# The last matrix product by Strassen's seven products, and the cap's transfer on another queue

## The chip, the cores and the metric

One core of a Trainium2 chip runs the kernel. The metric is device time in microseconds. The five engines are TensorE (PE in the rows; PEld is its weight load), VectorE (DVE), ScalarE (ACT), GpSimd (POOL, idle here) and SyncE (SP), which issues the transfers.

## The reference, cut to what matters

```python
scores = cap * tanh(scale * q @ k^T / cap)      # 4 x 12 heads, 448 tokens, 64 wide
x = softmax(scores) @ v                         # laid out as 1792 tokens x 768
u = (x @ w1) * (x @ w2)                         # 1792 x 1024
out = (u @ w3) @ w_out                          # 1792 x 768, w3 1024 x 1024, w_out 1024 x 768
```

The weights arrive as 64-bit floats, q, k, v and the cap as 32-bit floats.

## The kernel before, in words

The kernel computes C = w3 w_out first and then out = u C. Every matrix is split into a high part (the value rounded to the type that TensorE multiplies fast) and a low part (the rest); each product is three passes, high by high, high by low and low by high.

Stages: attention per pair of heads (S: scores, tanh, exp; V: values), beside it the splitting of w1 and w2 and the products pab; u goes to DRAM as eight blocks of 128 rows by 1792 tokens. From about 373 us the weights of the tail are split (`plan_piece`, L225 to L258: nine steps a piece on VectorE and ScalarE, 16 pieces of w_out and 24 of w3). C (`plan_C`, L880) takes eight blocks `it` of 128 rows, two halves of 384 columns, eight k steps `jt` and three passes: 384 matmuls. Each block needs its three pieces of w3, for which there are four buffers (two in a tile X, two in tiles W). ScalarE writes the high part of C (L904), VectorE the low part (L908). `plan_out` takes seven groups of 256 tokens: four loads of u from DRAM (L929), the high part on ScalarE (L939), the low part on VectorE (L942), two token blocks by two halves of columns, eight k steps, three passes (L968): 672 matmuls; ScalarE copies each result out of PSUM (L988) and SP stores it (L992).

The order of the work on each engine is fixed when the program is built. A planner (`Plan`) holds every step with an engine, a cost in ns, a key and the steps that it needs. It runs a clock for each engine, takes the engine that can start first and gives it the ready step with the lowest key (ready within a short wait: 91 ns for VectorE, 119 for ScalarE). A step with an alternative (the casts that make high parts: ScalarE or VectorE) goes to the engine that comes first. The result is an order for each engine's queue; on the chip a queue goes in that order and its head waits for what it needs. The dates that matter at the start: SP is free at 600 ns, VectorE at 1300, ScalarE at 1900 (before); an SP load costs 450 and lands 3300 later; the cap's lands 2000 after its issue; the scales made from the cap cost 750 on VectorE; a cast of a pair's kq costs 890 on ScalarE or 575 on VectorE for 960 columns, the low part 1070 on VectorE; pair 0's kq comes in two cuts of 576 and 384 columns with one date. Another engine learns of a step's end 130 ns (ScalarE) or 170 ns (VectorE) later; a step with an alternative counts as another engine's. Keys at the start: pair 0's load -6, the cap's -5.5, the scales' -5, pair 0's casts and low parts 1 and 2, pair 1's load 1.3 and its cast 8.3. Buffers are slots by tag: the i-th user of a tag with n slots needs all steps of user i - n. Pieces of the tail have keys from 500 up in the order w_out, w3 (`K0`, `CK`), C from 540, C's own high and low parts 500, the output from 700.

Of the kernel before, what the change touches and what calls it, by code (L numbers as in the profile page):

```python
# [137 lines left out]
def program(  # L138
# [651 lines left out]
    JG = ((0, 3), (3, 6), (6, 8))  # L790
    K0, CK = 500, 0.72
    w3t = []

    class OutPiece(Piece):
# [8 lines left out]
        def dest(self):  # L803
            if self.jt % 2 == 0 and self.nh == 0:
                pool, tag = (wop, f"wo{self.jt}") if self.jt < KF // 2 else (big, "W")
                t = pool.tile([P, 2, 2, DM], F32R, tag=tag, name=f"wo{self.jt}")
                self.wo.update((self.jt + i, t[:, i]) for i in range(2))
            return [
                self.wo[self.jt][:, x, self.nh * NH : (self.nh + 1) * NH] for x in range(2)
            ]  # L810

    class W3Piece(Piece):
        def __init__(self, it, z):
            self.it, (self.j0, self.j1) = it, JG[z]
# [4 lines left out]
            )  # L819

        def dest(self):
            if self.j0 == 0 and self.it == 0:
# [3 lines left out]
            elif self.j0 == 0 and self.it < NW3:  # L826
                t = big.tile([P, 2 * DF], F32R, tag="W", name=f"w3y{self.it}")
                w3t.append(t.rearrange("p (x a b) -> p x a b", x=2, b=P))
            y = w3t[self.it % NW3]
# [4 lines left out]
    NW3 = 4  # L834
    ct, wo = [], {}

    def plan_wo(jt, nh):
# [3 lines left out]
            nm, OutPiece(wo, jt, nh), key, (rawb, rtb), (("rawb", 6), ("rtb", 4)), 6,  # L841
            [f"O{jt // 2 * 2}_0high"] * (jt % 2 + nh > 0),
        )
        if jt % 2 == 0 and nh == 0:
            u = plan.tag("W", KF).take(done[nm + "high"]) if jt >= KF // 2 else []
            use["wo", jt // 2] = u
        use["wo", jt // 2].extend((done[nm + "high"], done[nm + "out"]))

    def w3_users(it):
        return [use["w3t", it], use["w3y", it % NW3]]  # L850

    def plan_w3(it, z):
        i = len(JG) * it + z
        nm = f"Z{it}_{z}"
        key = K0 + (2 * KF + i) * CK
        plan_piece(
            nm, W3Piece(it, z), key, (rawb, rtb), (("rawb", 6), ("rtb", 4)), 6,
            [f"Z{it}_0high"] * (z > 0) + ["Z0_0high"] * (it == 1),
        )
        t = done[nm + "high"]  # L860
        if z == 0:
            use["w3t", it] = plan.tag("w3t", NW3).take(t)
            if it == 0:
                use["w3y", 0] = use["w3y", 1] = plan.tag("X", 2).take(t)
            elif 2 <= it < NW3:
                use["w3y", it] = plan.tag("W", KF).take(t)
        for u in w3_users(it):
            u.extend((t, done[nm + "out"]))

    def plan_C(it):  # L870
        for nh in range(2):
            ns = slice(nh * NH, (nh + 1) * NH)
            box = {}
            for jt in range(KF):

                def emit(jt=jt, box=box, nh=nh, ns=ns):
                    if jt == 0:
                        box[0] = ps_f.tile([P, 512], F32, tag="f", name=f"pc{it}_{nh}")
                    for z, (a, c) in enumerate(((0, 0), (0, 1), (1, 0))):
                        nc.tensor.matmul(  # L880
                            box[0][:, :NH],
                            lhsT=w3t[it % NW3][:, a, jt, :],
# [5 lines left out]
                key = K0 + 40 + (it * 2 + nh) * KF + jt  # L888
                z = [i for i, x in enumerate(JG) if x[0] <= jt < x[1]][0]
                t = put(  # L890
                    f"C{it}_{nh}_{jt}", "PE", 521, key, emit,
                    [f"O{jt}_{nh}high", f"O{jt}_{nh}out", f"Z{it}_{z}high", f"Z{it}_{z}out"]
                    + [f"C{it}_{nh}_{jt - 1}"],
                )
                if jt == 0:
                    f = plan.tag("f", 3).take(t)
                use["wo", jt // 2].append(t)
                for u in w3_users(it):
                    u.append(t)

            def high(ns=ns, box=box, nh=nh):
                if it % 2 == 0 and nh == 0:
                    ct.append(big.tile([P, 2, 2, DM], F32R, tag="W", name=f"c_hl{it}"))
                nc.scalar.copy(ct[it // 2][:, it % 2, 0, ns], box[0][:, :NH])  # L904

            def low(ns=ns, box=box):
                h, l = (ct[it // 2][:, it % 2, x, ns] for x in range(2))
                nc.vector.tensor_tensor(l, box[0][:, :NH], h, op=ALU.subtract)  # L908

            t = put(f"D{it}_{nh}", "ACT", 400, K0, high, [f"C{it}_{nh}_{KF - 1}"])  # L910
            f.append(t)
            if it % 2 == 0 and nh == 0:
                t.key = key
                plan.tag("W", KF).take(t)
                t.key = K0
            t = put(f"L{it}_{nh}", "DVE", 470, K0, low, [f"D{it}_{nh}"])
            f.append(t)


    def plan_out(t):  # L920

        key = K0 + 200 + 10 * t
        hl, rs = {}, {}
        bs = range(2 * t * P // S, (2 * (t + 1) * P - 1) // S + 1)
        for m in range(0, KF, 2):

            def load(m=m):
                rs[m] = rawb.tile([P, 2, 2 * P], F32, tag="raw", name=f"ru{t}_{m}")
                nc.sync.dma_start(  # L929
                    rs[m],  # L930
                    u_dr[m : m + 2, :, 2 * t * P : 2 * (t + 1) * P].rearrange(
                        "m p t -> p m t"
                    ),
                )

            def high(m=m):
                if m == 0:
                    hl[0] = xp.tile([P, 2, KF, 2 * P], F32R, tag="X", name=f"uhl{t}")
                nc.scalar.copy(hl[0][:, 0, m : m + 2, :], rs[m])  # L939

            def low(m=m):
                nc.vector.tensor_tensor(  # L942
                    hl[0][:, 1, m : m + 2, :], rs[m], hl[0][:, 0, m : m + 2, :], op=ALU.subtract
                )

            x = put(
                f"q{t}_{m}", "SP", 800, key, load,
                [f"U{b}_{m + i}" for b in bs for i in range(2)], 2500,
            )
            r = plan.tag("rawb", 6).take(x)  # L950
# [192 lines left out]
```

## Time and profile before

| | us |
|---|---|
| median of three runs | 620.69 (618.08, 622.15, 620.69) |
| profiled execution | 617.45 |
| its span, first to last instruction | 615.7 |
| TensorE busy | 595.2 (97%) |
| VectorE busy | 357.3 (58%) |
| ScalarE busy | 312.9 (51%) |

The table gives one profiled execution beside the three timed ones. A busy share is a mean over stages; the stage's own windows tell more. TensorE's granted clock is given as a share of full speed (1.00 is 2.4 GHz).

### The profile page before, as it was taken

The page shows a single profiled execution, that of the slowest core. Times are in us where ns is not written, and L with a number is a line of the kernel's source. Part 1 is how long each engine was busy: PE and PEld are TensorE (multiplying, and loading weights), DVE is VectorE, ACT ScalarE, POOL GpSimd, SP SyncE. Part 2 cuts the span into 40 slices and gives each one's busy share as a digit, 9 for nine tenths or more (in the row PEclk, how much of TensorE's full clock was granted, in tenths as well). Part 3 has the DMA queues.
Part 4 walks back from the last instruction along what each step waited for, and adds up shares of the span by engine and source line. Part 5 has one row for each costly group of instructions (what it writes and reads, how often), then busy time and mean ns, then how long its engine had stood idle before and what let it go on. Part 6 is the DMA issues. An engine that isn't in the chain of part 4 may idle for free.

```text
span 615.7 us, 8843 instructions
## 1 busy us (share of the span) xinstructions
PE 595.2 (97%) x3336; PEld 479.4 (78%) x3336; DVE 357.3 (58%) x765; ACT 312.9 (51%) x485; POOL 0.2 (0%) x4
## 2 busy tenths in 40 slices
PE   5899999999999999999999998999999999999995
PEld 3443577666579777786777777999999999999995
DVE  3679999999991254562453356999999201111100
ACT  5999976797881146564554533444545212222200
POOL 0000000000000000000000000000000000000000
PEclk9999999999999999999999999999999999999998
DMA  7335554745551032222211116555645213332111
GB/s 239 99 113 179 170 188 135 240 130 159 192 168 46 15 97 77 81 72 75 76 48 47 31 50 231 161 181 181 188 141 157 92 39 107 121 120 79 47 52 43
DMA packets 39492, 71.87 MB, mean 117 GB/s; under 512 B 6034, under 2 KB 24082, under 8 KB 39442
## 3 DMA queue, kind: packets, MB, share of 16 engines
q1 hardware_dynamic: 39442, 71.23, 36.2%
q8 instruction: 28, 0.46, 0.3%
q14 instruction: 22, 0.18, 0.1%
HBM read 58.20 MB, written 12.93 MB: 116 GB/s over the span
## 4 chain that ended last, share of the span: by engine, by line
PE 77%; ACT 10%; DVE 5%; DMA 4%; issue 1%; SPq 1%; ACTq 0%; DVEq 0%
PE pab L741 34%; PE po L968 19%; PE pc L880 11%; PE s L397 6%; PE pv L446 5%; ACT p L411 5%; ACT p L408 4%; PE pv L436 1%; PE sum L472 1%; DMA kq<-in_kq_dram 1%; DMA raw_w<-in_moe_w_dram 1%; DMA r_dr<-z 1%; DMA raw_wo<-in_moe_w_out_dram 1%; DVE hl L364 1%; ACT t_w L230 1%
## 5 line engine op out<-in xcount | busy, mean ns | idle before, releaser
L741 PE MATMUL pab<-x,w_hl 128*128 128x448 f32 x1152 | 255.2, 374 | 2.7 <-ACT x L589 2.1
L741 PEld LDWEIGHTS pab<-x,w_hl 128*128 128x128 f32 x1152 | 212.6, 188 | 44.5 <-issue 20.7
L968 PE MATMUL po<-c_hl,uhl 128*128 128x384 f32 x672 | 116.6, 334 | 0.0
L968 PEld LDWEIGHTS po<-c_hl,uhl 128*128 128x128 f32 x672 | 116.5, 188 | 0.0
L408 ACT ACTIVATE p<-s,tsc_sb 128x896 f32<-128x896 f32 (+1 forms) x96 | 84.3, 916 | 38.3 <-PE s L397 37.9
L411 ACT ACTIVATE p<-p,ncap_sb,acap_sb 128x896 f32<-128x896 f32 (+1 forms) x96 | 97.7, 1047 | 0.5
L397 PE MATMUL s<-hl 64*128 64x448 f32 (+1 forms) x504 | 77.4, 392 | 8.5 <-ACT hl L360 4.4
L397 PEld LDWEIGHTS s<-hl 64*128 64x128 f32 (+1 forms) x504 | 50.9, 189 | 37.0 <-issue 17.8
L446 PE MATMUL pv<-p,v 128*64 128x448 f32 x288 | 61.3, 551 | 0.7 <-ACT p L411 0.7
L942 DVE TENSOR_TENSOR uhl<-ru,uhl 128x512 fp32r<-128x512 f32 x28 | 17.8, 686 | 74.4 <-ACT uhl L939 74.4
L988 ACT COPY ob<-po 128x384 f32<-128x384 f32 x28 | 13.4, 478 | 92.7 <-PE po L968 84.7
L230 ACT ACTIVATE t_w<-t_w,rebias 128x384 int32<-128x384 int32 (+1 forms) x56 | 33.0, 602 | 28.9 <-DVE t_w L225 28.8
L446 PEld LDWEIGHTS pv<-p,v 128*64 128x64 f32 x288 | 17.7, 136 | 31.9 <-issue 25.4
L766 DVE TENSOR_TENSOR u<-pab,u 128x448 f32<-128x448 f32 x32 | 19.6, 613 | 39.3 <-PE pab L741 36.1
L458 DVE TENSOR_TENSOR a<-p,p 128x896 f32<-128x896 f32 x24 | 26.1, 1088 | 27.3 <-PE sum L472 18.5
L880 PE MATMUL pc<-wo,w3x 128*128 128x384 f32 x192 | 33.6, 334 | 0.0
L880 PE MATMUL pc<-wo,w3y 128*128 128x384 f32 x192 | 33.6, 334 | 0.0
L880 PEld LDWEIGHTS pc<-wo,w3x 128*128 128x128 f32 x192 | 33.4, 188 | 0.0
L880 PEld LDWEIGHTS pc<-wo,w3y 128*128 128x128 f32 x192 | 33.3, 188 | 0.0
L233 DVE SCALAR_TENSOR_TENSOR t_w<-raw_w,t_w 128x384 int32<-128x384 int32 (+1 forms) x56 | 29.1, 527 | 2.6 <-ACT t_w L230 2.5
L241 DVE SCALAR_TENSOR_TENSOR raw_w<-raw_w 128x384 f32<-128x384 uint32 (+1 forms) x56 | 29.3, 528 | 0.1
L763 ACT COPY u<-pab 128x448 f32<-128x448 f32 x24 | 12.7, 529 | 31.5 <-PE pab L741 31.4
(59 smaller groups left out, 430.3 us busy)
## 6 DMA issues: line engine op xcount, KB each, us to landing
raw_w<-in_moe_w_dram SPq DMA_DIRECT2D x48, 384.0 KB
kq<-in_kq_dram SPq DMA_DIRECT2D x23, 480.0 KB
u_dr<-u SPq DMA_DIRECT2D x32, 224.0 KB
ru<-u_dr SPq DMA_DIRECT2D x28, 256.0 KB
v<-in_v_dram SPq DMA_DIRECT2D x24, 256.0 KB
raw_wo<-in_moe_w_out_dram SPq DMA_DIRECT2D x16, 384.0 KB
r<-r_dr SPq DMA_DIRECT2D x48, 112.0 KB
out_dram<-ob SPq DMA_DIRECT2D x28, 192.0 KB
```

The lines of the kernel that those rows point to most:

```text
L230: nc.scalar.activation(self.t, self.t, AF.Relu, bias=rebias, scale=4096.0)
L233: nc.vector.scalar_tensor_tensor(self.t, self.hi, SIGN, self.t, op0=ALU.bitwise_and, op1=ALU.bitwise_or)
L241: nc.vector.scalar_tensor_tensor(self.lo.bitcast(F32), self.lo.bitcast(U32), 2.0**-32, self.hi, op0=ALU.mult, op1=ALU.add,)
L397: nc.tensor.matmul(box[0][:, j, :S], lhsT=hl[at, a, ks], rhs=hl[at, c, QO:], start=(z == 0), stop=(z == 2),)
L408: nc.scalar.activation(p_t[pr, i], box[0][:, :w, :S], AF.Tanh, scale=tsc_sb)
L411: nc.scalar.activation(p_t[pr, i], p_t[pr, i], AF.Exp, scale=acap_sb, bias=ncap_sb)
L446: nc.tensor.matmul(box[0][j * D : (j + 1) * D, :S], lhsT=v_t[pr][:, 3 * j + i - 1, :], rhs=p_t[pr, i][:, j, :], start=False, stop=(i == 3) ...
L458: nc.vector.tensor_tensor(a_t[pr], p_t[pr, 1], p_t[pr, 2], op=ALU.add)
L741: nc.tensor.matmul(box[0][:, :S], lhsT=w_t[m][:, a, wi, kt, :], rhs=x_t[b][:, c, kt, :], start=(kt == 0 and z == 0), stop=(kt == KX - 1 an ...
L766: nc.vector.tensor_tensor(box[2][0], box[1][0][:, :S], box[2][0], op=ALU.mult)
L880: nc.tensor.matmul(box[0][:, :NH], lhsT=w3t[it % NW3][:, a, jt, :], rhs=wo[jt][:, c, ns], start=(jt == 0 and z == 0), stop=(jt == KF - 1 a ...
L968: nc.tensor.matmul(box[0][:, :NH], lhsT=hl[0][:, a, m, z * P : (z + 1) * P], rhs=ct[m // 2][:, m % 2, c, ns], start=(m == 0 and i == 0), s ...
```

## The change

The output stage computes u C with one level of Strassen's scheme in Winograd's form. C is cut into four quadrants (512 rows by 384 columns), u into four (896 tokens by 512 columns). Seven products of half size replace eight. The right operands are the quadrants B11, B21, B22 and T1 = C12 - C11, T3 = C22 - C12, T2 = C22 - T1, T4 = T2 - C21; the left ones are A11, A12, A22 and S1 = A21 + A22, S2 = S1 - A11, S3 = A11 - A21, S4 = A12 - S2.

C's row blocks are now computed in the order 0, 4, 1, 5, 2, 6, 3, 7 (`ITS`), so that a row of all four quadrants is there after every second block. Each result of C is copied out of PSUM whole (`D`), VectorE makes the four sums of a row as soon as they can be made, and each of the seven operands is split in high (ScalarE or VectorE) and low part (VectorE): 28 high, 28 low, 16 sums of 384 columns, where there were 16 high and 16 low. These steps have key 499, ahead of the pieces. w3 has two buffers in place of four, the split weights' temporaries three in place of four; one more w_out tile lies outside the W tiles, because the seven operands take seven of those eight.

The output stage takes seven blocks t of 128 tokens from the upper and 128 from the lower half of the tokens: four loads (one for each quadrant of u), four sums and seven splits of 512 columns, then the products in the order 1, 5, 2, 3, 6, 7, 4, each four k steps by three passes with 384 columns. Product 2 is added in the bank of product 1 and product 3 in that of 5, after copies of these (M1, M5) on ScalarE; the other sums of products are five steps of 384 columns on VectorE. Four stores a block leave as before.

At the start the cap's transfer is issued by ScalarE in place of SP; the planner's date for ScalarE's first step is 700 ns in place of 1900, and the scales' key is 2.5 in place of -5.

```diff
+    HF = KF // 2
+    ITS = [i // 2 + i % 2 * HF for i in range(KF)]
+    NRAW, NRT, NOB, NF = 6, 3, 9, 6
...
-            use["w3t", it] = plan.tag("w3t", NW3).take(t)
+            use["w3t", n] = plan.tag("w3t", 2).take(t)
...
+    RHS = {1: "B11", 2: "B21", 3: "B22", 4: "T4", 5: "T1", 6: "T2", 7: "T3"}
+    LHS = {1: "A11", 2: "A12", 3: "S4", 4: "A22", 5: "S1", 6: "S2", 7: "S3"}
+    ORDER = (1, 5, 2, 3, 6, 7, 4)
...
+            t = put(
+                f"D{c}", "ACT", 400, K0, lambda f=evac: f(nc.scalar.copy), [f"C{n}_{nh}_{KF - 1}"],
+                0, [("DVE", 450, lambda f=evac: f(nc.vector.tensor_copy))],
+            )
...
+            t = put(
+                f"h{name}_{k}", "ACT", 412, K0 - 1, lambda: high(nc.scalar.copy),
+                [after] + ["hB11_0"] * (not first), 0,
+                [("DVE", 269, lambda: high(nc.vector.tensor_copy))],
+            )
...
+            t = put(f"l{name}_{k}", "DVE", 470, K0 - 1, low, [f"h{name}_{k}"])
...
+        if not lower:
+            split("B11", c11, f"D{c11}")
+            combine(f"T1_{k}", c11, c12, c11, [f"D{c12}", f"lB11_{k}"])
+            split("T1", c11, f"T1_{k}")
+        else:
+            split("B21", c21, f"D{c21}")
+            split("B22", c22, f"D{c22}")
+            combine(f"T3_{k}", c12, c22, c12, [f"D{c22}", f"T1_{k}"])
+            combine(f"T2_{k}", c11, c22, c11, [f"D{c22}", f"lT1_{k}"])
+            split("T2", c11, f"T2_{k}")
+            split("T3", c12, f"T3_{k}")
+            combine(f"T4_{k}", c21, c11, c21, [f"T2_{k}", f"lB21_{k}"])
+            split("T4", c21, f"T4_{k}")
...
+                ru[nm] = rawb.tile([P, HF, P], F32, tag="raw", name=f"{nm}_{t}")
+                nc.sync.dma_start(
+                    ru[nm], u_dr[b * HF : (b + 1) * HF, :, at[a]].rearrange("m p t -> p m t")
+                )
...
+        for a, b in ((0, 0), (1, 0), (1, 1), (0, 1)):
+            load_quadrant(a, b)
+        l11 = split("A11", "A11", f"q{t}A11")
+        s3 = combine("S3", "A11", "A21", ALU.subtract, [f"q{t}A11", f"q{t}A21"], new=True)
+        s1 = combine("A21", "A21", "A22", ALU.add, [s3, f"q{t}A22"])
+        split("S1", "A21", s1)
+        l12 = split("A12", "A12", f"q{t}A12")
+        s2 = combine("A11", "A21", "A11", ALU.subtract, [s1, s3, l11])
+        s4 = combine("A12", "A12", "A11", ALU.subtract, [s2, l12])
+        split("S4", "A12", s4)
+        split("S2", "A11", s2)
+        split("S3", "S3", s3)
+        split("A22", "A22", f"q{t}A22")
...
+                    for z, (a, c) in enumerate(((0, 0), (0, 1), (1, 0))):
+                        nc.tensor.matmul(
+                            box[banks[m]][:, :NH],
+                            lhsT=hl[g][:, i, a, k, :],
+                            rhs=bt[RHS[m]][:, k, c, :],
...
+        copy(f"e{t}M1", "U", "X", 1, 0)
+        copy(f"e{t}M5", "M5", "Z", 5, 1)
+        copy(f"e{t}11", "o11", "X", 2, 2)
+        store("o11", 0, 0, f"e{t}11")
+        add(f"e{t}U", "U", "Y", "U", ALU.add, [end(6), f"e{t}M1"])
+        add(f"e{t}12", "o12", "Z", "U", ALU.add, [end(3), f"e{t}U"], new=4)
+        store("o12", 0, 1, f"e{t}12")
+        add(f"e{t}V", "U", "V", "U", ALU.add, [end(7), f"e{t}12"])
+        add(f"e{t}22", "M5", "U", "M5", ALU.add, [f"e{t}V", f"e{t}M5"])
+        store("M5", 1, 1, f"e{t}22")
+        add(f"e{t}21", "U", "W", "U", ALU.subtract, [end(4), f"e{t}22"])
+        store("U", 1, 0, f"e{t}21")
...
-            nc.sync.dma_start(cap_sb, cap.to_broadcast([P, 1]))
+            nc.scalar.dma_start(cap_sb, cap.to_broadcast([P, 1]))
...
-        plan.free.update(PE=1500.0, ACT=1900.0, DVE=1300.0, POOL=900.0, SP=600.0)
+        plan.free.update(PE=1500.0, ACT=700.0, DVE=1300.0, POOL=900.0, SP=600.0)
...
-        put("cap0", "SP", 450, -5.5, load_cap, lat=2000)
-        put("cap", "DVE", 750, -5, scales, ["cap0"])
+        put("cap0", "ACT", 450, -5.5, load_cap, lat=2000)
+        put("cap", "DVE", 750, 2.5, scales, ["cap0"])
```

## Rows read from the trace of the kernel before

**Rows 1.** The page: the chain's shares; groups with count | busy us, mean ns.

```profile
PE 77%; ACT 10%; DVE 5%; DMA 4%; issue 1%; SPq 1%; ACTq 0%; DVEq 0%
L741 PE MATMUL pab<-x,w_hl 128*128 128x448 f32 x1152 | 255.2, 374 | 2.7 <-ACT x L589 2.1
```

**Rows 2.** Windows: length, busy of PE, PEld, DVE, ACT, POOL, then clock, DMA share, GB/s.

```profile
9.50:78.60 69.10, 64.53 (x417) 32.43 (x415) 56.51 (x106) 68.77 (x97) 0.00 (x0) 1.00 0.49 156
...
426.30:476.20 49.90, 49.90 (x290) 49.90 (x289) 49.38 (x141) 23.98 (x50) 0.00 (x0) 1.00 0.52 159
476.20:492.90 16.70, 16.70 (x98) 16.70 (x97) 4.69 (x8) 4.10 (x8) 0.00 (x0) 1.00 0.31 95
...
492.89:609.39 116.50, 116.49 (x673) 116.17 (x671) 13.04 (x21) 23.78 (x48) 0.00 (x0) 1.00 0.23 78
609.39:615.70 6.31, 0.00 (x0) 0.00 (x0) 0.00 (x0) 0.48 (x1) 0.00 (x0) 0.72 0.12 39
```

**Rows 3.** The chain in order of time, the tail: start, us, what.

```profile
426.31 66.58 PE pc L880 x384
492.89 116.50 PE po L968 x672
...
609.46 0.48 ACT ob L988
```

**Rows 4.** Groups by line in the tail: count | busy us, mean ns | idle before.

```profile
L942 DVE TENSOR_TENSOR uhl<-ru,uhl 128x512 fp32r<-128x512 f32 x28 | 17.8, 686 | 74.4 <-ACT uhl L939 74.4
L939 ACT CAST uhl<-ru 128x512 fp32r<-128x512 f32 x28 | 15.6, 620 | 1.9 <-DMA ru<-u_dr 1.9
...
L255 ACT CAST w3x<-t_w 128x384 fp32r<-128x384 f32 (+1 forms) x11 | 5.2, 484 | 6.1 <-DVE t_w L233 6.0
...
L255 ACT CAST w3y<-t_w 128x384 fp32r<-128x384 f32 (+1 forms) x9 | 4.3, 475 | 4.3 <-DVE t_w L233 4.2
```

**Rows 5.** VectorE in order of time, the tail: start, us, line, operation.

```profile
405.93 0.35 DVE L255 CAST wo<-t_wo 128x384 fp32r<-128x384 f32 x1
406.20 0.55 DVE L241 SCALAR_TENSOR_TENSOR raw_wo<-raw_wo 128x384 f32<-128x384 uint32 x1
...
471.29 0.55 DVE L908 TENSOR_TENSOR c_hl<-pc,c_hl 128x384 fp32r<-128x384 f32 x1
471.76 0.41 DVE L233 SCALAR_TENSOR_TENSOR t_w<-raw_w,t_w 128x256 int32<-128x256 int32 x1
472.09 0.68 DVE L942 TENSOR_TENSOR uhl<-ru,uhl 128x512 fp32r<-128x512 f32 x1
472.69 0.29 DVE L238 TENSOR_SCALAR raw_w<-raw_w 128x256 int32<-128x256 int32 x1
...
474.36 0.42 DVE L258 SCALAR_TENSOR_TENSOR w3y<-raw_w 128x256 fp32r<-128x256 f32 x1
```

**Rows 6.** The chain in order of time, the start: start, us, what.

```profile
1.65 0.42 SPq L1009
...
2.12 6.46 DMA kq<-in_kq_dram
...
9.50 0.64 ACT p L408
```

**Rows 7.** ScalarE and VectorE in order of time, the start; in brackets idle before, releaser.

```profile
3.65 1.08 ACT L360 CAST hl<-kq 128x576 fp32r<-128x576 f32 x2 [1.64 <-DMA kq<-in_kq_dram]
...
7.33 1.23 DVE L364 TENSOR_TENSOR hl<-kq,hl 128x576 fp32r<-128x576 f32 x2
...
8.60 0.99 ACT L360 CAST hl<-kq 128x960 fp32r<-128x960 f32 x1 [3.86 <-DMA kq<-in_kq_dram]
...
15.80 0.65 DVE L360 CAST hl<-kq 128x960 fp32r<-128x960 f32 x1
```

**Rows 8.** Window of the start, columns as in rows 2.

```profile
3.20:5.80 2.60, 0.74 (x1) 0.28 (x1) 0.00 (x0) 1.08 (x2) 0.00 (x0) 1.00 0.72 108
```

**Rows 9.** The chain in order of time, a load of weights: start, us, what.

```profile
368.97 4.43 DMA raw_wo<-in_moe_w_out_dram
```

More of the change, by code (lines that the diff above doesn't have):

```diff
@@ L894, in plan_C @@
                 )
                 if jt == 0:
-                    f = plan.tag("f", 3).take(t)
+                    f = plan.tag("f", NF).take(t)
                 use["wo", jt // 2].append(t)
-                for u in w3_users(it):
+                for u in (use["w3t", n], use["w3y"]):
                     u.append(t)
[L901 to L904, printed above, removed]
@@ L917, in plan_C, with evac @@
-            f.append(t)
-    def plan_out(t):
[L922 to L928, printed above, removed]
+            c = f"c{lower}{nh}_{k}"
+            def evac(cp, box=box, c=c):
+                cf[c] = obp.tile([P, NH], F32, tag="ob", name=c)
+                cp(cf[c], box[0][:, :NH])
@@ L946, in plan_out @@
+            bs = range(at[a].start // S, (at[a].stop - 1) // S + 1)
             x = put(
[L947 to L955 removed]
@@ new lines, in load_quadrant, with combine, emit @@
+                f"q{t}{nm}", "SP", 800, key, load,
+                [f"U{i}_{m}" for i in bs for m in range(b * HF, (b + 1) * HF)], 2500,
+            )
+            x.spare = SPARE
+            use[nm, t] = plan.tag("rawb", NRAW).take(x)
+        def combine(to, a, b, op, needs, new=False):
+            def emit():
+                if new:
+                    ru[to] = rawb.tile([P, HF, P], F32, tag="raw", name=f"{to}_{t}")
+                elif to != a and to != b:
+                    raise ValueError(to)
+                nc.vector.tensor_tensor(ru[to], ru[a], ru[b], op=op)
+            x = put(f"s{t}{to}{a}{b}", "DVE", 600, key, emit, needs)
+            if new:
+                use[to, t] = plan.tag("rawb", NRAW).take(x)
+            for y in {to, a, b}:
+                use[y, t].append(x)
+            return f"s{t}{to}{a}{b}"
@@ new lines, in add, with emit @@
+        def add(nm, to, bank, b, op, needs, new=None):
+            def emit():
+                if new is not None:
+                    result(to)
+                x = box[bank][:, :NH] if bank in box else ob[bank]
+                a, c = (ob[b], x) if op == ALU.subtract else (x, ob[b])
+                nc.vector.tensor_tensor(ob[to], a, c, op=op)
+            x = put(nm, "DVE", 470, key - 5, emit, needs)
+            if new is not None:
+                x.key = key + 2 * new
+                use[to, t] = plan.tag("ob", NOB).take(x)
+                x.key = key - 5
+            for y in {to, bank, b}:
+                use[y, t].append(x)
```

254 lines of the change are left out of this document (147 added, 107 removed).

## The prediction

> **What bounds the kernel now.** I began with the page: 77% of the chain that ended last is TensorE [rows 1]. The busy times by stage say where an engine's time is the kernel's time: from 426.3 us to 609.4 TensorE has no gap, while in the last of these stretches VectorE is busy 13.04 of 116.50 us and ScalarE 23.78 [rows 2]. The chain in order of time shows the two stages that the change touches as unbroken matmuls: 66.58 us for 384 of C, 116.50 us for 672 of the output, 173.4 ns each in both, then a copy and a store [rows 3]. VectorE needs a second look: it is busy 49.38 of 49.90 us up to 476.20, then 4.69 of 16.70 [rows 2]: full through most of C, with 12.0 us free at its end. The start is read apart: its chain is a transfer of kq, a cast, then tanh and exp, and ScalarE is busy 68.77 of 69.10 us from 9.50 to 78.60 [rows 6, 2], so a late first tanh is a late kernel.
>
> **The output stage.** Seven products of four k steps and three passes, for seven row blocks: 588 matmuls instead of 672, same shape (128x128 by 128x384). 84 x 173.4 ns = **14.57 us off**, if TensorE stays without gaps. The work that must keep up, per block of 84 x 173.4 ns = 14.57 us: on VectorE 7 low parts and 4 sums of 512 columns at 0.60 (start to start of such a row and the next), and 5 result sums of 384 at 0.47 [rows 5]: 6.6 + 2.35 = 8.95 us. On ScalarE 7 casts of 620 ns [rows 4] and 3 copies of 480 [rows 3]: 5.8 us. Both lie beside matmuls. SP issues four u loads and four stores a block, as many as before; the loads read 512-byte runs where they read 1 KB, with the DMA engines 0.23 busy in this stretch [rows 2]. Products 2 and 3 start in a bank that must have been copied out; another product (12 x 173.4 ns = 2.08 us) lies between, and a copy starts 0.07 us after its matmuls (609.46 against 492.89 + 116.50) and takes 0.48 [rows 3]: nothing. If that cover goes (ScalarE stuck ahead of the copy), each block pays the copy, 0.5 us. The last result is a VectorE sum (0.55 us, the row of C's low part, which also reads PSUM) in place of a copy (0.48) [rows 5, 3]: +0.07. The store behind it is the same size.
>
> **The C stage.** TensorE's 384 matmuls stay. VectorE gets 28 low parts for 16 and 16 sums that are new: 28 x 0.47 = 13.2 us. The first left parts (11 x 0.60 = 6.6) stand for 8 low parts of u (4.8): +1.8. Some high parts go to VectorE: ScalarE took 20 of the 24 casts of w3 [rows 4], VectorE the others; a sixth of 28 at 0.27 [rows 5] is 1.2. Together 16.2 against 12.0 us free: 4.2 us of work slides past the end of C. That is covered by need: of the seven right operands T2, T3 and T4 enter 8.3, 10.4 and 12.5 us into the first block. The harder date is w3's last piece, since sums go ahead of pieces in the planner's keys. It was finished at 474.78 [rows 5], and the last i block of C starts at 426.31 + 7 x 8.32 = 484.6. Ahead of it go the sums' steps of k = 0 and 1 (22) and the first three of k = 2, where 10 low parts of C had gone before: 15 more (7.0 us), and 1 us of casts, less 4 low parts of u that are no longer ahead (2.4): 480.4. Two w3 buffers instead of four mean that this block's high parts wait for 426.31 + 6 x 8.32 = 476.2, which is earlier still. Behind such a waiting high part on ScalarE stand the next piece's rebias and, behind that, VectorE's sign step; the planner knows the date, and ScalarE has room. So I take 0; margin 4.2 us. Below, the bound is 0 as well, for TensorE has no gap there to close [rows 2]; above I take 4 us, the overflow as a stall.
>
> **The start.** SP loses a 0.42 us issue that stands ahead of pair 1's kq (0.47 with the gap before it) [rows 6]. ScalarE issues it while it waits anyway: its first cast starts at 3.65 after 1.64 us of idling [rows 7]. What the move does to the order costs more than the issue. The planner decides by its own dates who casts pair 1. Before: ScalarE, free at 5.37, because kq1 is dated 5.25; the trace agrees, with the 960-column cast on ScalarE at 8.60, after two small ones [rows 7]. Now kq1 is dated 0.6 + 2 x 0.45 + 3.3 = 4.80, VectorE has done the cap's scales (3.28 to 4.03), ScalarE is busy till 4.88, and pair 0's low part is dated 5.01. So VectorE takes pair 1's cast **ahead of pair 0's low part**, and in the real run stands in its queue until kq1 lands. It landed at 8.58; 0.47 earlier at best. Then the cast, 0.65, the first low part about 0.7 (1.23 for the two) [rows 7], two score matmuls about 0.75 (twice the 374 ns of a 448-column one [rows 1]): tanh at 10.2 to 10.7 instead of 9.50. I take the middle, **+0.9**. The cast that leaves ScalarE is no second gain: it ended where tanh began. The bounds: if VectorE did pair 0's low part while it waits for the cap, and then the scales, these would end not at 7.33 but earlier by the cap's earlier issue, 1.65 against 0.73 at best, and tanh would start at about 6.5: -3.0. Upward +1.2.
>
> On the transfer itself the trace shows a stretch from 3.2 to 5.8 us, behind pair 0's load and ahead of kq1's landing, in which the DMA engines were 0.72 busy but moved 108 GB/s [rows 8], against 156 at 0.49 busy from 9.50 on [rows 2]. The cap's, issued between the two loads [rows 6], is the likely cause, and it is now issued beside pair 0's load. I take nothing for that, since kq1 was behind both before and is so now. The Trainium skill ("DMA: Bandwidth & Descriptors", Issuing engines are not separate DMA queues) says that transfers from different issuers share the same 16 engines and interleave, so that another queue saves issue time only. By that, the cap's move is worth the issue slot and no more, and its place in the order is open; this is rival 3.
>
> **Sum.** The profiled execution took 617.45 us (615.7 span, 1.75 around it): 617.45 - 14.57 + 0.07 + 0.9 + 0 = 603.9. The median of the three runs, 620.69, lies 3.24 above it; on that scale **607.1 us**.
>
> **Rivals.** *1. VectorE bounds C.* If the planner gives VectorE most of the 28 casts and half the 16 evacuations (28 x 0.27 + 8 x 0.47 = 11 us, not 1.2), the last w3 piece comes near 490 and TensorE waits about 5 us: 612. For it: VectorE is full to 476 [rows 2]. Against: ScalarE is busy only 23.98 of those 49.90 us [rows 2], and took most casts so far.
>
> *2. Slower: the preparation loop of the output stage is longer than a block.* Six raw slots hold the loads and S3 of a block, so block t+1's A21 can be loaded only when A11 of block t has been through S3, S1, S2 and S2's split, and A12 only after A22's. By durations: issue 0.4, landing at most 4.43 (a load of weights with five others behind it [rows 9]), three sums and one low part at 0.69, a cast at 0.62 [rows 4]: 8.2 us, and with the five result sums between them (2.75) 11. It is the bound from 14.57 us; over 1% slower needs 14.57 + (13.6 + 6.2)/7 = 17.4 us a block, for instance if a blocked head of VectorE's queue, a result sum waiting for TensorE, keeps the next block's preparation behind it. Then each block ends with a gap: 627 or more. Behind a waiting load on SP stand the stores, whose nine slots last two blocks. Against: the planner orders by dates, and its costs fit the trace (512-column low part 600 against 0.60 measured). A rule bears on it, in the Trainium skill ("Perfetto Trace Analysis", Optimization Strategy): a gap that repeats on the engine that should be full can mean too few buffers for the next tile. No row of before shows such a gap.
>
> *3. The cap's transfer shifts the loads.* If its small packets interleave with pair 0's load instead of standing between pair 0 and pair 1, kq1 can land earlier or later by up to the stretch in which they held the engines, 2.6 us [rows 8]; VectorE's cast waits for it, so the tanh moves with it: 604.5 or 609.7.
>
> *4. The start gains:* the -3.0 above instead of +0.9: 603.2.
>
> **Chances.** Forecast 0.70 (603 to 610), rival 1 0.12 (609 to 614), rival 2 0.06, rival 3 0.04, rival 4 0.05; the last 0.03 are gaps of 1 to 2.5 us a block, half of rival 2, 614.5 to 625. The range takes in rival 4, the forecast and most of rival 1, with about 1 us for the median of few runs: 602 to 613. A measurement of this kernel tells about 1% (6.2 us) from no change: faster by more than that 0.87, within it 0.07 (the half of rival 2, the tail of 1 and 0.02 of the forecast's own for what I don't see), slower 0.06.
>
> **What would show it.** In the profile after: 588 matmuls of the products in about 102 us without idle time, and about 66.6 us for C; if TensorE idles in C with releaser VectorE (w3's low part), rival 1; if a gap comes back with every block, rival 2, and the granted clock (1.00 in these stretches, 0.72 after the last matmul [rows 2]) should then be looked at too. At the start: a 960-column cast of kq on VectorE ahead of the first low part, and tanh after 10 us. The forecast is wrong if the products' stretch exceeds 110 us or the first tanh comes before 8.

## The result and the profile after

| | before | after |
|---|---|---|
| median of the runs, us | 621.42 (618.08 to 622.26, 4 runs) | 612.53 (611.64 to 613.37, 4 runs) |
| profiled execution, us (span) | 617.45 (615.7) | 611.64 (609.8) |

The ratio is 0.9862, 95% interval [0.9838, 0.9886]: faster by 1.4%, 8.9 us by the medians. The forecast was 607.1; the time lies inside the range of 602 to 613, at its upper end. The profiled spans differ by 5.9 us, and this is where they do: C begins 8.72 us later (435.03 against 426.31 [rows 3]), C itself takes 0.06 more, the output stage 14.56 less, and what is behind it 0.11 less. The profiled execution of the kernel before is a short one of its kind (617.45 us against medians of 620.5 to 621.5), so the spans differ by less than the medians.

The tail of the chain in order of time after (start, us, what); it answers to [rows 3] and [rows 9]:

```profile
375.73 3.12 DMA raw_wo<-in_moe_w_out_dram
379.41 0.61 ACT t_wo L230
380.50 54.53 PE pab L741 x252
435.03 66.64 PE pc L890 x384
501.66 101.94 PE m L1084 x588
603.63 0.55 DVE U L1131
```

The 588 matmuls of the products stand without a gap, 173.4 ns each, and C has none either. Ahead of C the chain goes the same way as before the change: the first load of w_out, a rebias on ScalarE (L230, a step of the splitting of the weights), a copy of pab (the first result of the last block of u) out of PSUM, and the 252 matmuls. But the copy comes 5.5 us later. Before, behind the load at 368.97 [rows 9]:

```profile
373.88 0.04 ACT t_wo L230
...
374.40 0.52 ACT u L763
```

After, the load starts at 375.73 and the rebias at 379.41. The windows (length, busy of PE, PEld, DVE, ACT, POOL, clock, DMA share, GB/s) of the entry to the tail, of C in two parts, of the output stage and of the end:

```profile
375.00:380.00 5.00, 2.25 (x6) 1.18 (x5) 0.71 (x3) 0.59 (x2) 0.00 (x0) 0.52 0.62 200
380.00:385.00 5.00, 4.50 (x12) 4.03 (x13) 3.29 (x9) 2.54 (x6) 0.00 (x0) 0.50 0.88 319
...
435.03:484.93 49.90, 49.90 (x289) 49.90 (x289) 47.23 (x129) 23.80 (x50) 0.00 (x0) 1.00 0.38 111
484.93:501.66 16.73, 16.73 (x98) 16.64 (x97) 16.73 (x41) 9.80 (x19) 0.00 (x0) 1.00 0.23 65
501.66:603.60 101.94, 101.93 (x589) 101.61 (x587) 65.45 (x116) 33.71 (x63) 0.00 (x0) 1.00 0.35 109
603.60:609.79 6.19, 0.00 (x0) 0.00 (x0) 0.55 (x1) 0.00 (x0) 0.00 (x0) 0.80 0.20 71
```

From 375 to 385 us TensorE's granted clock is 0.52 and 0.50, half speed, the lower of its two levels (1.2 GHz). The kernel before, in the same ten microseconds:

```profile
375.00:380.00 5.00, 5.00 (x25) 4.64 (x26) 3.91 (x11) 2.51 (x5) 0.00 (x0) 1.00 0.59 232
380.00:385.00 5.00, 5.00 (x26) 4.64 (x25) 5.00 (x14) 0.52 (x1) 0.00 (x0) 1.00 0.55 157
```

What TensorE waited for there, in order of time (in brackets idle before, releaser), first before, then after:

```profile
372.67 1.75 PE L741 MATMUL pab<-x,w_hl 128*128 128x448 f32 x6 [1.56 <-ACT x L589]
374.97 10.20 PE L741 MATMUL pab<-x,w_hl 128*128 128x448 f32 x49 [0.55 <-ACT u L763]
```

```profile
374.73 2.52 PE L741 MATMUL pab<-x,w_hl 128*128 128x448 f32 x6 [1.99 <-ACT x L589]
380.50 11.75 PE L741 MATMUL pab<-x,w_hl 128*128 128x448 f32 x45 [3.25 <-ACT u L763]
```

The wait for the copy of pab is 3.25 us instead of 0.55. ScalarE's rows after say why the copy is late:

```profile
379.41 0.61 ACT L230 ACTIVATE t_wo<-t_wo,rebias 128x384 int32<-128x384 int32 x1 [4.74 <-DVE t_wo L225]
379.94 0.51 ACT L763 COPY u<-pab 128x448 f32<-128x448 f32 x1
```

The copy stands in ScalarE's queue behind the rebias of w_out's first piece, where it stood before too, and that piece was loaded late: the six loads that it is the first of were issued from 375.73, right behind the last work on x (VectorE, 374.70 for 0.64), and before the change from 368.97. In the built program the first of these loads waits for TensorE alone before, and for TensorE, VectorE and four transfers after. So the 8.72 us fall into three: the last x came 2.06 later (the six matmuls on it start at 374.73, not 372.67); from there to the next matmul 5.77 us instead of 2.30, 3.47 more, all of it set by the late copy; and the 252 matmuls 54.53 us instead of 51.34, 3.19 more.

The start of the chain in order of time after, and then VectorE and ScalarE there; they answer to [rows 6, 7]:

```profile
1.67 5.40 DMA kq<-in_kq_dram
7.67 0.76 DVE hl L364
```

```profile
7.10 0.66 DVE L360 CAST hl<-kq 128x960 fp32r<-128x960 f32 x1 [1.08 <-DMA kq<-in_kq_dram]
7.67 2.29 DVE L364 TENSOR_TENSOR hl<-kq,hl 128x576 fp32r<-128x576 f32 x3
...
5.23 1.08 ACT L360 CAST hl<-kq 128x576 fp32r<-128x576 f32 x2 [2.79 <-DMA kq<-in_kq_dram]
9.63 0.64 ACT L408 ACTIVATE p<-s,tsc_sb 128x448 f32<-128x448 f32 x1 [3.32 <-PE s L397]
```

VectorE takes pair 1's 960-column cast ahead of pair 0's low part, as forecast; the first tanh is at 9.63, where 10.2 to 10.7 had been forecast. Pair 1's kq landed at 7.07 (8.58 before), pair 0's first cast began at 5.23 (3.65 before).

### The profile page after: what moved, and what is told of

Its sections match the earlier page's. It is cut to its first block, busy times and chain, and to the rows that moved or that the text cites. A ratio compares the mean times of both kernels' runs of the same rounds, so it can differ in the third digit from the quotient of the medians.

```text
span 609.8 us, 8833 instructions
## 1 busy us (share of the span) xinstructions
PE 585.6 (96%) x3252; PEld 467.7 (77%) x3252; DVE 423.3 (69%) x888; ACT 330.9 (54%) x516; POOL 0.2 (0%) x4
## 4 chain that ended last, share of the span: by engine, by line
PE 80%; ACT 8%; DMA 6%; DVE 4%; issue 1%; SPq 1%; ACTq 0%; DVEq 0%
PE pab L741 36%; PE m L1084 17%; PE pc L890 11%; PE s L397 7%; PE pv L446 6%; ACT p L411 3%; ACT p L408 3%; PE pv L436 2%; DMA r_dr<-z 2%; DMA r<-r_dr 1%; PE sum L472 1%; DMA raw_w<-in_moe_w_dram 1%; DMA kq<-in_kq_dram 1%; SPq L559 1%; DMA raw_wo<-in_moe_w_out_dram 1%
## 5 line engine op out<-in xcount | busy, mean ns | idle before, releaser
L741 PE MATMUL pab<-x,w_hl 128*128 128x448 f32 x1152 | 259.7, 378 | 6.8 <-ACT x L589 3.5
L741 PEld LDWEIGHTS pab<-x,w_hl 128*128 128x128 f32 x1152 | 214.8, 190 | 50.9 <-issue 20.7
L890 PE MATMUL pc<-wo,w3x 128*128 128x384 f32 x384 | 66.8, 334 | 0.0
L890 PEld LDWEIGHTS pc<-wo,w3x 128*128 128x128 f32 x384 | 66.6, 188 | 0.1
L1084 PE MATMUL m<-bB,lx 128*128 128x384 f32 x252 | 45.9, 334 | 0.0
L230 ACT ACTIVATE t_w<-t_w,rebias 128x384 int32<-128x384 int32 (+1 forms) x56 | 32.9, 601 | 21.4 <-DVE t_w L225 21.4
L1084 PEld LDWEIGHTS m<-bB,lx 128*128 128x128 f32 x252 | 43.9, 188 | 0.0
L1034 ACT CAST lx<-A 128x512 fp32r<-128x512 f32 x32 | 19.6, 620 | 28.6 <-DVE A L1010 11.0
L360 DVE CAST hl<-kq 128x960 fp32r<-128x960 f32 x22 | 14.4, 655 | 25.1 <-PE s L397 23.9
L1084 PE MATMUL m<-bT,lx 128*128 128x384 f32 x168 | 31.4, 334 | 0.0
L1084 PE MATMUL m<-bT,lw 128*128 128x384 f32 x168 | 30.2, 334 | 0.0
```

The source lines that it names most:

```text
L230: nc.scalar.activation(self.t, self.t, AF.Relu, bias=rebias, scale=4096.0)
L741: nc.tensor.matmul(box[0][:, :S], lhsT=w_t[m][:, a, wi, kt, :], rhs=x_t[b][:, c, kt, :], start=(kt == 0 and z == 0), stop=(kt == KX - 1 an ...
L890: nc.tensor.matmul(box[0][:, :NH], lhsT=w3t[n % 2][:, a, jt, :], rhs=wo[jt][:, c, ns], start=(jt == 0 and z == 0), stop=(jt == KF - 1 and ...
L1084: nc.tensor.matmul(box[banks[m]][:, :NH], lhsT=hl[g][:, i, a, k, :], rhs=bt[RHS[m]][:, k, c, :], start=(new and k == 0 and z == 0), stop=( ...
```

## The experiments

The theory after the result, P: the new pools (a third w_out tile, nine result buffers instead of three) push the raw weights' buffers over memory that the last attention pair still uses (among its tiles xf, from which x is made, and r); the first load then waits for that pair, the rebias for the load, the copy of pab for the rebias, and TensorE's clock falls in the wait. Rivals: Q, the place is harmless and the new order of the tail is the cause; O, the order in ScalarE's queue could hide the late load; S, the cap's move makes the start later; K, the clock's share of the loss is its own.

Each median stands beside one of the kernel before on the same chip: 620.61 for e1 to e4, 620.5 for e5 to e8, 621.5 for e9 and e10. Across these three groups, and against the changed kernel's 612.53, only the ratios compare:

| run | median, us | ratio to before, interval | C starts at |
|---|---|---|---|
| e1_pools | 608.01 | 0.9781 [0.9761, 0.9802] | 431.37 |
| e2_before_moved | 625.55 | 1.0079 [1.0057, 1.01] | 431.53 |
| e3_order | 607.87 | 0.9789 [0.9772, 0.9807] | 429.82 |
| e4_cap_back | 610.84 | 0.984 [0.9824, 0.9856] | 433.45 |
| e5_before_cap | 622.02 | 1.0029 [1.0014, 1.0043] | 427.83 |
| e6_pools_cap_back | 606.32 | 0.9779 [0.9754, 0.9804] | 431.25 |
| e7_pools_cast_act | 606.39 | 0.9778 [0.9756, 0.9799] | 431.23 |
| e8_fill | 603.8 | 0.9741 [0.9718, 0.9765] | 426.88 |
| e9_after_fill | 609.97 | 0.9822 [0.9801, 0.9842] | 431.31 |
| e10_all | 606.0 | 0.9752 [0.9731, 0.9773] | 428.12 |

**The pools opened first** (changed kernel, instruction order the same):

```
-        wop = fin.enter_context(tc.tile_pool(name="wop", bufs=1))
-        obp = fin.enter_context(tc.tile_pool(name="obp", bufs=NOB))
         rawb = ...
         rtb = ...
+        wop = fin.enter_context(tc.tile_pool(name="wop", bufs=1))
+        obp = fin.enter_context(tc.tile_pool(name="obp", bufs=NOB))
```

> The changed kernel with one edit: the pools of the raw weights and of their temporaries are opened ahead of the w_out and result pools, so that they lie over memory that attention has left long ago. The order of instructions on every engine is that of the changed kernel. Theory P (place): the first load of w_out no longer waits for the last pair's x, is issued at about 370 us and not at 375.7, TensorE's gaps between 370 and 381 fall from 6.1 us to about 2 to 3, the granted clock stays 1.00, C starts at 427 to 429 and not at 435.0; time 604 to 606, some 6 to 8 us under the changed kernel's 612.5. Rival Q (queue): SP was late in any case, because a small transfer of the softmax sums landed 1.7 us later and SP stood behind it; then the load is issued at 374 or later and the time is 610 or more.

608.01, ratio 0.9781. SyncE's and TensorE's rows of this kernel in order of time:

```profile
372.83 3.17 SPq L218 DMA_DIRECT2D raw_wo<-in_moe_w_out_dram  x6
...
376.41 15.90 PE L741 MATMUL pab<-x,w_hl 128*128 128x448 f32 x69 [2.36 <-ACT x L589]
```

The loads go out behind the last r transfer again, with no wait for x, and no wait for the copy of pab is left. 0.8% of before came back, some 5 us, less than expected: the wait for x stayed, 2.36 us, the clock in the five microseconds behind it was 0.66, and the attention itself ended 1.7 us later than in the changed kernel's trace (last sums at 364.27 against 362.54).

**The kernel before with its raw buffers pushed on:**

```
-        obp = fin.enter_context(tc.tile_pool(name="obp", bufs=3))
+        obp = fin.enter_context(tc.tile_pool(name="obp", bufs=17))
```

> The kernel before with one edit: the result pool has 17 buffers for 3, of which the plan still uses 3 at a time; nothing else, and the raw weights' pool moves to where the changed kernel has it. Theory P: the first load of w_out waits for the last x and is issued at 374 to 376 us instead of 369, TensorE's clock falls to half for a few us, C starts 5 to 8 us later, the time is 626 to 629 against about 621. Rival Q: no change, 620 to 622.

625.55, ratio 1.0079: slower, a little less than expected, with nothing changed but where the buffers lie. In the built program they lie at the addresses that they have after the change, and the first load waits for the same engines and transfers as there. Chain of this kernel in order of time, then its windows:

```profile
372.94 3.62 DMA raw_wo<-in_moe_w_out_dram
376.56 0.60 ACT t_wo L230
377.63 53.90 PE pab L741 x252
```

```profile
370.00:375.00 5.00, 2.38 (x8) 1.10 (x6) 1.25 (x2) 0.56 (x1) 0.00 (x0) 0.80 0.29 65
375.00:380.00 5.00, 2.37 (x6) 2.15 (x7) 1.51 (x5) 1.55 (x3) 0.00 (x0) 0.50 1.00 375
380.00:385.00 5.00, 5.00 (x19) 4.49 (x18) 5.00 (x14) 2.07 (x4) 0.00 (x0) 0.68 0.34 101
```

The same load, the same rebias, the same fall of the clock and slow 252 matmuls (53.90) as after the change, in a kernel without the seven products. C starts 5.22 us later. P is shown: the place alone does it. Q, by which the place is harmless, is refuted.

**The planner told of the late load** (changed kernel; the first six loads get the last x as a need, so that the planner orders ScalarE by the true date):

```
+    LATE = {f"O{j}_{h}" for j in range(3) for h in range(2)}
...
+            if st == "load" and nm in LATE:
+                need = [f"N2{NPAIR - 1}"]
```

> The changed kernel, pools where it has them, with one edit: the planner is told that the first six loads of w_out need the last pair's x. The loads stay late (375 to 376 us); ScalarE's copy of the first result of the last block of u then stands ahead of the first rebias in its queue. If the loss comes from the queue's head (the copy behind a rebias that waits for a late load), the copy runs at 376 to 377 and not at 379.9, TensorE is idle about 3 us less there, its clock falls less or not at all, and C starts at 428 to 430; time 605 to 608. If the late load itself is the loss (VectorE gets the weights late), C starts at 433 or later and the time stays at 611 or more.

607.87, ratio 0.9789. The loads are as late as in the changed kernel (376.26), but the copies now stand ahead of the rebias, and only the wait for x is left. TensorE's rows of this kernel (line numbers are three higher):

```profile
375.26 9.97 PE L744 MATMUL pab<-x,w_hl 128*128 128x448 f32 x38 [2.13 <-ACT x L592]
...
484.28 8.27 PE L893 MATMUL pc<-wo,w3x 128*128 128x384 f32 x46 [1.05 <-DVE w3x L259]
```

So what a late load costs is what stands behind it in ScalarE's queue; O holds, the order alone recovers what the place does. The second row is the forecast's rival 1 in small: TensorE waits 1.05 us in C for a late piece of w3 from VectorE.

**The cap back on SyncE's queue** (changed kernel):

```
-            nc.scalar.dma_start(cap_sb, cap.to_broadcast([P, 1]))
+            nc.sync.dma_start(cap_sb, cap.to_broadcast([P, 1]))
...
-        put("cap0", "ACT", 450, -5.5, load_cap, lat=2000)
-        put("cap", "DVE", 750, 2.5, scales, ["cap0"])
+        put("cap0", "SP", 450, -5.5, load_cap, lat=2000)
+        put("cap", "DVE", 750, -5, scales, ["cap0"])
```

> The changed kernel with the cap's transfer back on SP and the planner's dates and keys of before for it; the Strassen part stays. By my forecast the move of the cap costs about 0.9 us, so this kernel would be 611.6; by the trace the first tanh was 0.13 us later than before, so 612.4. If the other queue also slows the small transfers of the softmax sums, the first r transfers land as in the kernel before and the kernel is up to 2 us faster, 610.5. The start's order is that of before: pair 1's cast on ScalarE, tanh at 9.5 us. C starts at 433 to 435.

610.84, ratio 0.984 against 0.9862 of the changed kernel: 0.22% or 1.4 us, less than the two intervals tell apart. **The cap's move alone**, in the kernel before (the same lines the other way):

> The kernel before with nothing of the change but the cap's transfer on ScalarE's queue. Theory S (the start's order costs; taken from the changed kernel against the same with the cap back, 0.9862 to 0.9840, and from TensorE's place at the last attention sums, 101.5 us against 100.0): 1.2 to 1.6 us slower than before, 621.8 to 622.2 against 620.6, first tanh at 9.6 to 10.2 us instead of 9.50 and every later stage of the attention later by the same. Rival: the 1.4 us is chance between runs and the cap's place costs nothing: 620.3 to 621.0. Second rival: the earlier start of the first query pieces wins: under 620.

622.02, ratio 1.0029 [1.0014, 1.0043] of twelve runs: slower by 0.9 to 2.7 us. That the move costs is shown. That it costs by making the start later, as S has it, is not. VectorE's row and ScalarE's at the start of this kernel, then TensorE's at the entry to the tail, a window and the chain there:

```profile
7.21 0.66 DVE L360 CAST hl<-kq 128x960 fp32r<-128x960 f32 x1 [0.85 <-DMA kq<-in_kq_dram]
...
9.74 0.63 ACT L408 ACTIVATE p<-s,tsc_sb 128x448 f32<-128x448 f32 x1 [3.25 <-PE s L397]
```

```profile
373.05 1.75 PE L741 MATMUL pab<-x,w_hl 128*128 128x448 f32 x6 [1.56 <-ACT x L589]
...
375.00:380.00 5.00, 4.89 (x17) 4.47 (x18) 3.21 (x9) 2.11 (x5) 0.00 (x0) 0.68 0.65 257
...
375.11 52.72 PE pab L741 x252
```

The first tanh is 0.24 us later than before, the last sums of the attention 0.37 (362.65 against 362.28), and C 1.52 (427.83 against 426.31). In between the granted clock fell, behind a wait for x that is as long as before (1.56 us), and the 252 matmuls took 1.38 us more. So most of what this one execution lost is not the start's. Whether the twelve runs lost their time in the same place is open: their mean clocks (0.992 to 0.996) hardly differ from those of the seventeen beside them (0.993 to 0.996).

Over the profiled executions with that order of VectorE (after, e1, e3, e5, e9) the first tanh is at 9.63, 9.88, 9.41, 9.74 and 10.13, a mean of 9.76; with the cap on SyncE's queue (before, e2, e4, e6, e8, e10) at 9.50, 8.34, 9.47, 10.01, 8.33 and 9.58, a mean of 9.21. The two groups overlap: single profiles of the start differ by more than the move costs.

**Both undone: pools first and the cap back** (e1's edit and e4's):

> The changed kernel with the raw weights' pools opened ahead of the new ones (so that they keep off attention's last tiles) and the cap back on SP's queue. If the two costs (place of the pools 5 us, cap 1.4 us) are apart and add up: 606.4 to 606.8, C starting near 429.8 us of the span. Rival: the place and the start share a cause, or e1's later attention was the pools' order and not the cap's: 607.7 to 608.3 as with the pools alone.

606.32 is the number expected, but the ratio, 0.9779 [0.9754, 0.9804], equals e1's, and the chips differ; in its profile the first tanh came at 10.01 and C began at 431.25. That the two gains add up is neither shown nor refuted.

**Pair 1's cast kept on ScalarE, cap on ScalarE's queue, pools first:**

```
-                [("DVE", 575 * w, lambda f=high: f(nc.vector.tensor_copy))],
+                [("DVE", 575 * w, lambda f=high: f(nc.vector.tensor_copy))] * (pr != 1),
```

> As the changed kernel with the pools opened first, the cap on ScalarE's queue, but pair 1's cast kept on ScalarE, so that VectorE comes to pair 0's low part first. Theory S1 (the order of VectorE's first casts is the cost of the start): first tanh at 8.2 to 9.0 us, 606.0 to 607.0. Rival S2 (the other order at the start or the transfers' order costs, not VectorE's turn): 607.7 to 608.3, with tanh earlier and the time given back before the last attention pair.

606.39 lies in the range of S1, but on a chip where the kernel before was at 620.5; the ratio, 0.9778, is that of e1 (0.9781). VectorE's first row on kq in this kernel:

```profile
6.13 0.76 DVE L364 TENSOR_TENSOR hl<-kq,hl 128x576 fp32r<-128x576 f32 x1
```

It comes 1.5 us earlier than after the change (7.67) and the first tanh with it, at 8.09; but the last sums of the attention stand at 365.29, later than in e1's trace (364.27). In this profile the tanh is the earliest of all, and what was won there was lost before the last pair, as S2 had it: from the first tanh to the last sums it takes 357.2 us, against 354.4 in e1 and 352.7 to 354.6 in the other kernels. There a late first tanh is a late end of the attention, as the prediction has it; here the two come apart. Where the time was lost was not followed further.

**Six matmuls more, in the wait for x** (e6 with them):

```
+    if (b, m, wi, kt) == (B - 1, 0, 0, KX - 1):
+        fill = ps_f.tile([P, 512], F32, tag="f", name="fill")
+        for i in range(6):
+            nc.tensor.matmul(fill[:, :S], lhsT=w_t[m][:, 0, wi, 0, :],
+                             rhs=x_t[b][:, 0, 0, :], start=True, stop=True)
```

> The kernel with the pools first and the cap back, with six more matmuls on TensorE whose result is not used, put where it waits for the last pair's x (2.36 us idle with the pools alone; six at about 370 ns are 2.2 us). Theory K (after that gap the clock, 0.66 in the 5 us behind it, makes the next 250 matmuls 2 to 3 us longer): the clock stays at 1.00, the stretch to C's start takes 52 us instead of 54.96, and the time is 2.0 to 2.8 us under the kernel without them. Rival: the clock falls all the same or the added matmuls delay the needed ones by as much: within 0.7 us of the kernel without them. On the other side: x comes earlier than the six are done, 0.5 to 1.5 us slower.

603.8, ratio 0.9741 [0.9718, 0.9765]; e6 on the same chip 606.32. TensorE's rows and the window, in this kernel:

```profile
370.63 1.38 PE L743 MATMUL fill<-x,w_hl 128*128 128x448 f32 x6
373.54 1.74 PE L748 MATMUL pab<-x,w_hl 128*128 128x448 f32 x6 [1.53 <-ACT x L589]
375.54 16.68 PE L748 MATMUL pab<-x,w_hl 128*128 128x448 f32 x81 [0.26 <-ACT u L770]
```

```profile
375.00:380.00 5.00, 4.74 (x24) 4.14 (x23) 4.20 (x12) 3.06 (x7) 0.00 (x0) 1.00 0.70 276
```

The wait is still there, only partly filled, but the clock stays at 1.00, and the 252 matmuls take 51.34 us, as before the change (53.81 in e6). It is 2.5 us by the medians, as K expected; the two intervals just overlap, the two traces do not leave it open. The profiled spans differ by 4.3 us (606.3 against 602.0); 2.0 of that is the end of the attention (last sums at 361.28 against 363.25), which in this execution began early (first tanh 8.33 against 10.01).

**The same in the changed kernel, all its waits left in place** (six matmuls in the wait for x, nine in the wait for the copy; the edit is the one above, with a second place at m = 1, wi = 0, kt = 0):

> The changed kernel, its order and its memory as they are, with fifteen more matmuls on TensorE whose result is not used: six where it waits for the last pair's x (1.99 us idle in the changed kernel's trace) and nine where it waits for the copy of pab (3.25 us idle). They take away no wait and so show the clock's part of the loss alone. Theory K: the clock stays at 1.00 from 375 to 385 us (0.52 and 0.50 in the changed kernel), the 252 matmuls behind take 51.3 to 51.8 us instead of 54.53, and the time is 2.4 to 3.2 us under the changed kernel's, 609.3 to 610.1. Rival: the loss is all in the waits, and the matmuls behind are slow for another reason (the first weights' traffic, 0.88 of the DMA engines' time in these 5 us): 612 to 613, with the stretch still at 54 us.

609.97, ratio 0.9822 [0.9801, 0.9842] against 0.9862 [0.9838, 0.9886] of the changed kernel: the intervals touch, so the trace has to decide. The chain of this kernel and a window:

```profile
375.62 3.25 DMA raw_wo<-in_moe_w_out_dram
379.98 51.34 PE pab L749 x252
```

```profile
380.00:385.00 5.00, 5.00 (x25) 4.65 (x26) 4.05 (x11) 2.52 (x5) 0.00 (x0) 1.00 0.73 281
```

The load is as late as after the change, and from the first of the last six matmuls on x to the 252 it is 5.77 us as there (374.21 to 379.98), but the 252 matmuls run at full clock: 3.19 us of the 8.72 are the clock's, 2.5 by the ratios. The Trainium skill ("TensorE: Matmul & The Clock Gate", HAM oscillation — how this bites in real kernels) describes a kernel in which the wait for a transfer between bursts of matmuls brings the array's clock to half, so that the next burst starts cold; by that, a wait can cost more than its length. This case's runs agree: behind the two waits of 1.99 and 3.25 us the 252 matmuls took 3.19 us more.

**All together** (e8 with e3's dates):

> All that helped, together: pools first, cap back on SP's queue, the six added matmuls at the wait for the last pair's x, and the first six weights' loads given to the planner as needing that x, so that the copies of pab come ahead of the first rebias. If the 0.26 us idle for the copy is all that the order can still give: 603.2 to 603.8, 0 to 0.5 us under the kernel without the planner's dates (0.9741 of before). Rival: the later loads cost C its w3 pieces (a wait of 1.05 us stood there in the run with the planner's dates): 604 to 605.

606.0, ratio 0.9752 [0.9731, 0.9773], against 0.9741 [0.9718, 0.9765] of e8: no gain. The loads are early again (371.64), and yet a wait in C is there, as the rival had it, if not by its cause; TensorE's row:

```profile
482.48 8.27 PE L900 MATMUL pc<-wo,w3x 128*128 128x384 f32 x46 [0.79 <-DVE w3x L259]
```

The lowest ratio of these runs is that of e8_fill: 2.6% under before, where the change as it was gave 1.4%.

## Why the prediction was right or wrong

**The output stage: right.** 101.94 us for 588 matmuls against 116.50 for 672 [rows 3], 14.56 off where 14.57 had been worked out, and no gap: rival 2 did not occur. VectorE was busy 65.45 us in it, 9.35 a block where 8.95 were reckoned.

**The end: right in its place.** The last operation is VectorE's sum, 0.55 us against ScalarE's copy of 0.48 [rows 3]; what is behind the last matmul is 0.11 us shorter in the spans, not 0.07 longer, below what one execution tells.

**C: the time right, the margin and the date of need not.** 66.64 us, no gap. That VectorE's work would overflow the end of C was right: it is busy 16.73 of the last 16.73 us, where it had been busy 4.69 of 16.70 [rows 2]. But w3's last piece was ready at 497.37, which is 62.3 us behind C's start, and 54.1 had been reckoned, with 58.3 as the date of need. The 4.2 us of margin were not there. The groups on VectorE in C after say what stood ahead:

```profile
L959 DVE TENSOR_TENSOR c<-c,c 128x384 f32<-128x384 f32 x13 | 7.1, 548 | 1.8 <-ACT c L915 1.8
L938 DVE TENSOR_TENSOR bT<-c,bT 128x384 fp32r<-128x384 f32 x13 | 7.0, 546 | 0.0
...
L938 DVE TENSOR_TENSOR bB<-c,bB 128x384 fp32r<-128x384 f32 x11 | 6.0, 547 | 0.3 <-ACT bB L934 0.3
...
L255 DVE CAST w3x<-t_w 128x384 fp32r<-128x384 f32 x6 | 2.1, 350 | 0.0
...
L934 DVE CAST bB<-c 128x384 fp32r<-128x384 f32 x4 | 1.4, 348 | 0.0
```

Ahead of the last piece of w3 stood 23 of these low parts and the 13 sums, 36 steps where 25 had been reckoned: 11 more at 0.47 us are 5.2 us. Two results of C that VectorE copied out (0.54 us each) and two steps of u had not been reckoned there at all. The casts of C's high parts, 1.4 us, were near the 1.2 reckoned; those of w3 are six where VectorE had four before. Seven of C's steps slid past its end, 3.3 us of work where 4.2 had been reckoned. So the amount of work was near the forecast, and its order was not.

TensorE did not idle in this run because the date of need was wrong too, on the other side. The prediction took the start of the last block; but the last piece holds only k steps 6 and 7 of it (`JG` in the kernel), and as the program is built the planner put steps of the block's second half ahead. The first matmul that reads the piece's high part is number 361 of C's 384, at 360 x 173.5 ns or 62.5 us behind C's start (497.5), and the first that reads its low part is two further on (497.8). The low part was ready at 497.37. The margin was half a microsecond, and not the 4.2 us reckoned.

Rival 1 did not occur here, but 1.05 and 0.79 us of it stand in e3 and e10. From the first load of w_out to C's start they have 53.6 us (376.26 to 429.82) and 56.5 (371.64 to 428.12), where the changed kernel has 59.3 (375.73 to 435.03) and e8, without a wait in C, 57.3 (369.59 to 426.88). Whether this shorter time or the planner's other dates cause the wait was not told apart.

**The start: the order right, its price not settled.** Forecast +0.9 us, between -3.0 and +1.2. Measured alone the move costs 0.9 to 2.7 us (e5): the forecast is at the lower end of that, and the middle, 1.8, is above its upper bound; and how much of it is the start's is open. The step took pair 1's kq to land 0.47 us earlier at best; it landed 1.5 earlier, and pair 0's was later: its first cast began at 5.23 instead of 3.65. The transfers shifted against each other, as rival 3 had it, and that moved the tanh by less than forecast (9.63; 9.41 to 10.13 over five profiles). The rule that the prediction weighed there, in the Trainium skill ("DMA: Bandwidth & Descriptors", Issuing engines are not separate DMA queues), says that transfers of different issuers interleave: that the two loads shifted agrees with it. That the other queue saves issue time only does not cover what was measured, since the move cost time.

**The step that was missing** is in the sum itself: output, C, start and end were priced, and everything between the start and C was carried over unchanged. No term stood for the memory that the new pools take. The prediction did read the row on which it turned, the load of w_out at 368.97 in the chain [rows 9], but used it as a duration and did not ask what makes that load wait and what stands behind it on ScalarE. It was on the chain before already, with the rebias and the copy behind it. What it cost: of 8.72 us at C's start, 3.47 are the wait for the copy and 3.19 the clock behind it. With the pools opened first the ratio is 0.9781 (e1), and the forecast as a ratio, 607.1 to 620.69, is 0.978.

The other 2.06 us are the last x's delay, of which 0.26 is the attention's end (sum at 362.54 against 362.28). 1.58 us of the rest came where SyncE waited for r_dr, the softmax sums' way through DRAM, of the pair before the last (after, SyncE in order of time):

```profile
362.38 0.33 SPq L555 DMA_DIRECT2D r_dr<-z  x1
...
365.80 1.15 SPq L559 DMA_DIRECT2D r<-r_dr  x2
```

From the issue of r_dr<-z to that of r<-r_dr it takes 3.42 us after, 1.84 or 1.85 in the three kernels without the seven products, and 2.7 to 3.4 in those with them, except in e7, where it is 1.84 too. So it is neither the cap's queue (3.35 in e4, 1.84 in e5) nor the pools' place (3.29 in e1, 1.85 in e2), and the seven products alone do not bring it about. The order of these instructions and what they wait for are the same. This cause stays open.

The forecast was therefore right in what the change does at its own places, and by the medians 5.4 us too low (7.7 on the profiled scale, 603.9 against 611.64) because of what it displaces. That the time still lies in the range is luck: the range reached 613 for rival 1, a wait in C, and that did not occur; a loss of its size came from another place.

## What to carry to other kernels

A change that adds buffers moves every pool opened after them: for each first transfer into the moved memory, ask what used that memory last, and what stands in the queues behind whoever waits for it. Open the pool whose first load is earliest over the memory that comes free earliest, or tell the planner the true date; either gave back about 5 us here. And price a wait on TensorE with the slower matmuls behind it, not by its length alone.

## What the runs showed of the hardware

- The granted clock fell to half behind short waits. In e7 one idle stretch of 1.77 us on TensorE, in e3 one of 2.13, in e1 one of 2.36 were followed by five microseconds at a mean of 0.66 to 0.68. The length of that one stretch does not decide it: behind 1.56 us the clock stayed at 1.00 before the change and fell, to a mean of 0.68, in e5. Six added matmuls (0.23 us apart) in such a wait kept it at 1.00, although 1.53 us of idling were left (e8).
- Moving one tiny transfer to another engine's queue delayed a large one: the first cast of the first kq pair starts at 5.04 to 5.23 us in the six profiles with the cap on ScalarE's queue, and at 3.50 to 3.84 in the six with it on SyncE's. The second pair's load, which leaves one issue earlier, landed at 7.07 us instead of 8.58 in the first two profiles; over all twelve the two groups overlap there.
